# Attention and an MLP on one core: sums of x, stores of weight sums and x's loads are put elsewhere in the queues

## The chip, the cores and the metric

The kernel runs on one core of a Trainium2 chip. The metric is device time in microseconds (us), the median of several runs. A core has five engines that run side by side, each with its own queue of instructions in a fixed order: TensorE (PE; its weight loads are shown apart as PEld), VectorE (DVE), ScalarE (ACT), GpSimd (POOL) and SyncE (SP), which here only issues DMAs. ScalarE and GpSimd issue DMAs too, between their other instructions. An engine waits at the head of its queue until what the next instruction needs is there; everything behind it waits along.

## The reference

What must be computed is an attention whose mask comes from hashes, and an MLP on its output.

```python
# q, k, v: (4, 8, 768, 64); proj: (64, 6); w_in: (512, 2048); w_out: (2048, 512)
q_bits = (np.einsum('bhsd,dk->bhsk', q, proj) > 0)
k_bits = (np.einsum('bhsd,dk->bhsk', k, proj) > 0)
mask = q_bucket[:, :, :, None] == k_bucket[:, :, None, :]      # all six bits equal
scores = np.where(mask, scale * q @ k.T, -1e9)
x = (softmax(scores) @ v)            # to (3072, 512): heads side by side
h = x @ w_in
out = (np.maximum(h, 0) + alpha * np.minimum(h, 0)) @ w_out
```

## The kernel before

**Two parts.** Attention goes over 16 pairs of heads (4 batches of 4 pairs); pair `pi` is one turn of the loop at L1190. It takes the first 320 us or so. Then the MLP runs over 4 batches of x. Its products are cut into blocks of two by two and made with seven products in place of eight, so sums and differences of blocks are needed: of w_in (index `wsi`, kept in the DRAM buffer `w_in_s`), of w_out, of x and of the MLP's inner values g. The sums for the MLP's first batch are made during attention.

**One pair on TensorE.** Twelve cells of scores (L782), each six matmuls: two with the hash bits (`qb`, `kb`), four with q and k. A cell is 128 keys by 384 queries; the cells go key block by key block, and within one over the two halves of the queries, so the first cell needs the bits of k's first half and of q's first half, the second q's second half, and k's second half only from the seventh cell on. Then come the hash products of the next pair (L732), the products with v (L815) and the column sums of the exponentials (L828, tile `sm`). Scores, hash products and column sums share three PSUM buffers (`two_banks`, L691) in turn: a pair's third cell takes the buffer of the last pair's column sums, which VectorE's transpose `st` (L842) must have read; the fourth cell takes the buffer of the first, which ScalarE's exp (L785) must have read.

**Around it.** ScalarE makes the exp of every cell, the signs of the hash products (L736), squares for a check (L719) and parts of the weights' rounding (`weight_abs`, L604 and L608). VectorE adds the exponentials of six key blocks (`add_first`, L793, adds blocks 0 and 1 and so needs four cells' exps; then L801, L797, L798, L804), turns q and k (L712), finishes the last pair's division (`divide`, L832: `st`, reciprocals, `vs`, then the transpose `dn` of `rr`, then x at L860) and rounds the weights (L614, L620, L645, L648). Between the reciprocals and `dn`, GpSimd copies four pieces of `rr` (L851, L852). `divide` of pair `pi - 1` is called behind the scores of pair `pi`; the function `weight_begin` is called inside it, between GpSimd's copies and `dn`, and holds the turn of k, the rounding of a weight piece and `add_first`.

**Sums of w_in.** A group of four rounded pieces gives four sums (`one`, L667, on GpSimd) and four stores (`store`, L672, SyncE). They wait in the list `sums_due`; `weight_sums(1)` takes one sum from it, and is called twice in a pair: within `divide` ahead of the copies of `rr`, and behind the pair's second rounding. A store in the list goes with the next call. There are four such groups.

**DMAs.** The bits of a pair are packed by eight small DMAs from `hr` to `qb` and `kb` (L743): two issued by ScalarE, six by GpSimd. SyncE loads q and k of pair `pi + 3` (L515, four DMAs each), v of pair `pi + 2` (L491), stores x of each pair to DRAM (`x_s`, L861), loads blocks of x (`load_x`, L875) and of w_in's sums (`load_w`, L891) for the MLP.

**Order.** `do(...)` keeps an instruction in program order among those of its engine that are marked so. DMAs without it are placed by the scheduler, as the loads of q, k and v and the stores of w_in's sums here.

Of the kernel before, what the change touches and what calls it, by code (L numbers as in the profile page):

```python
# [407 lines left out]
def fast_path(  # L408
# [12 lines left out]
    nc = tc.nc  # L421
    P = 128
    B, H, S, D = q.shape
    NB = proj.shape[1]
# [4 lines left out]
    NC = S // P  # L429
# [4 lines left out]
    CW = CH * P  # L434
# [8 lines left out]
    do = tc.keep_in_program_order  # L443
    PE, DVE, ACT, POOL = nc.tensor, nc.vector, nc.scalar, nc.gpsimd
# [10 lines left out]
    NPAIR = len(pairs)  # L455
# [18 lines left out]
    w_in_s = dram.tile([NI, P, NM, 2, P], F32, name="w_in_s")  # L474
# [8 lines left out]
    nat, tr, bits = {}, {}, {}  # L483
    accp, accd, av, vsum, sums = {}, {}, {}, {}, {}

    def load(pi, name):
        b, hp = pairs[pi]
        src = {"q": q, "k": k, "v": v}[name]
        if name == "v":
            t = pool.tile([P, 2, NC * D], F32, name=f"vn{pi}", tag="vn")  # L490
            nc.sync.dma_start(t, src[b, 2 * hp : 2 * hp + 2].rearrange("h (p c) d -> p h (c d)", c=NC))  # L491
            nat[name, pi] = t
        elif pi and name in BY_BLOCKS:
            load_blocks(pi, name)
        else:
            load_part(pi, name, slice(0, NC), nc.sync)
# [102 lines left out]
    def weight_abs(i, engine=None):  # L599
        i = order[i]  # L600
        lo, hi = halves(i)
        wx[i] = pool.tile([P, 512], F32, name=f"wx{i}", tag="wx")
        wr[i] = pool.tile([P, 512], I32, name=f"wr{i}", tag="wr")
        do(ACT.activation(wr[i], lo, AF.Copy, scale=2.0 ** -29))  # L604
        if engine is DVE:
            do(DVE.tensor_scalar(wx[i].bitcast(U32), hi, 0x7FFFFFFF, None, op0=ALU.bitwise_and))
            return
        do(ACT.activation(wx[i], hi.bitcast(F32), AF.Abs))  # L608
# [7 lines left out]
    def weight_parts(i):  # L616
        i = order[i]
        x = wx[i].bitcast(U32)
        turned = i < HW and i % 4 == 3
        do(DVE.tensor_scalar(  # L620
            x, x, 3, 0x40000000 if turned else 0xC0000000, op0=ALU.logical_shift_left, op1=ALU.bitwise_xor,
        ))
# [25 lines left out]
        do(DVE.tensor_tensor(dst.bitcast(I32), x, r, op=ALU.add))  # L648
        return (dst if i < HW else dst[:, 0])[:, :1]

    sums_due = []

    def weight_group(i):

        i = order[i]
        if i >= HW:
            n, m = divmod(i - HW, 2)
            if m == 1:
                nc.sync.dma_start(w_out_r[:, :, n].rearrange("m p d -> p m d"), wst[HW + n])
            return  # L660
        n, m = divmod(i, 4)
        if m < 3:
            return
        w = wst[n]

        def one(to, a, op, c):
            do(POOL.tensor_tensor(w[:, to], w[:, a], w[:, c], op=op))  # L667

        def store():
            c, kk = divmod(n, 2)  # L670
            for ii in range(4):
                nc.sync.dma_start(w_in_s[4 * c + ii][:, :, kk], w[:, :, ii])  # L672


        for x in ((3, 5, 2), (5, 0, 5), (4, 3, 0), (6, 1, 4)):
            sums_due.append((one, (x[0], x[1], ALU.subtract, x[2])))
        sums_due.append((store, ()))

    late_sum = const.tile([P, 1], F32, name="late_sum")

    def weight_sums(count, after=None):

        if sums_due and after is not None:
            do(POOL.tensor_copy(late_sum, after))
        while sums_due and count:
            fn, x = sums_due.pop(0)
            count -= fn.__name__ == "one"
            fn(*x)


    def two_banks(name):  # L691
# [34 lines left out]
    def hash_bits(pi):  # L726

        ps = two_banks(f"hs{pi}")[:, 0, :CW]
        for half in range(2):
            for n, name in enumerate("kq"):  # L730
                c = D * n + 32 * half
                do(PE.matmul(  # L732
                    ps[c : c + 32], wh2, tr[name, pi][:, half * CW : (half + 1) * CW], start=True, stop=True,
                ))
        raw = pool.tile([P, CW], BF16, name=f"hr{pi}", tag="hr", bufs=1)
        do(ACT.activation(raw, ps, AF.Sign, bias=hb2))  # L736
        bits["q", pi], bits["k", pi] = qbs[pi % 2], kb
        for half in range(2):
            for n, name in enumerate("kq"):
                for s in range(2):  # L740
                    c = D * n + 32 * half + NB * s
                    queue = nc.gpsimd if half or name == "q" else nc.scalar
                    queue.dma_start(  # L743
                        bits[name, pi][D * s : D * s + 2 * NB, half * CW : (half + 1) * CW], raw[c : c + 2 * NB],
                    )

    def hash_first(half):

# [25 lines left out]
    def scores(pi, cells):  # L774
        for kc, g in cells:
            sc = two_banks(f"sc{pi}_{kc}_{g}")
            ks = slice(kc * P, (kc + 1) * P)
            qs = slice(g * CW, (g + 1) * CW)
            for what, first in ((bits, True), (tr, False)):
                for s in range(2):  # L780
                    r = slice(D * s, D * s + D)
                    do(PE.matmul(  # L782
                        sc[:, s, :CW], what["k", pi][r, ks], what["q", pi][r, qs], start=first, stop=not first,
                    ))
            do(ACT.activation(pts[kc][:, g, :, :CW], sc[:, :, :CW], AF.Exp, scale=SCALE / DOWN))  # L785
# [5 lines left out]
    def add_first(pi):  # L791
        accp[pi] = pool.tile([P, 2 * NCH, CW], F32, name=f"accp{pi}", tag="accp", bufs=1)
        do(DVE.tensor_tensor(accp[pi], p(0), p(1), op=ALU.add))  # L793
# [77 lines left out]
    def load_x(b, *ns):  # L871
        for n in ns or range(4):
            m, kh, ch = ((0, 0, 0), (1, 1, 0), (2, 1, 1), (5, 0, 1))[n]
            t = mid.tile([P, 2, CW], F32, name=f"x{b}_{m}", tag=f"x{m}", bufs=1)
            pinned(b == 0, nc.sync.dma_start(  # L875
                t, x_s[b, 2 * kh : 2 * kh + 2].rearrange("k p s -> p k s")[:, :, ch * CW : (ch + 1) * CW],
            ))
            x_m[b, m] = t

    def sum_x(b, n, engine):  # L880

        to, a, c = ((3, 5, 0), (5, 2, 5), (4, 2, 3), (6, 4, 1))[n]
        if to != 5:
            x_m[b, to] = mid.tile([P, 2, CW], F32, name=f"x{b}_{to}", tag=f"x{to}", bufs=1)
        do(engine.tensor_tensor(x_m[b, to], x_m[b, a], x_m[b, c], op=ALU.subtract))
# [303 lines left out]

    for pi in range(NPAIR):  # L1190
        i = 2 * pi

        def weight_begin():
            if pi == 1:
                turn_blocks(2, "q")
            if pi + 1 < NPAIR:
                turn_blocks(pi + 1, "k")
            weight_clamp(i)
            weight_parts(i)
            add_first(pi)  # L1200

        if pi:
            scores(pi, CELLS)
            divide(pi - 1, weight_begin)
        else:
            rest = [c for c in CELLS if c not in ahead]
            scores(pi, rest[:4])
            weight_abs(0, DVE)
            scores(pi, rest[4:])
            add_first(pi)  # L1210
            weight_clamp(0)
            weight_parts(0)
        if pi in (8, 10, 12, 14):
            sum_x(0, (8, 10, 12, 14).index(pi), DVE)
        weight_sum(i)
        weight_group(i)
        load_weight(i + 3)
        if pi == 0:
            weight_abs(1, DVE)
        weight_clamp(i + 1)  # L1220
        add_third(pi)
        add_last(pi)
        add_total(pi)
        weight_parts(i + 1)
        weight_sums(1, weight_sum(i + 1))
        weight_group(i + 1)
        load_weight(i + 4)
        if pi + 1 < NPAIR:
            hash_bits(pi + 1)
            do(ACT.activation(tr["q", pi + 1], tr["q", pi + 1], AF.Copy, scale=DOWN))  # L1230
        if 0 < pi < NPAIR - 2:
            turn_blocks(pi + 2, "q")
        attend(pi)
        if pi + 1 == NPAIR:
            now = ff1(0, 0)
            now.step(1)
        totals(pi)
        if pi + 1 == NPAIR:
            now.step(5)
            divide(pi)  # L1240
        else:
            weight_abs(i + 2)
        if pi + 2 < NPAIR:
            load(pi + 2, "v")
        if pi in (9, 11, 15):
            load_w((9, 11, 15).index(pi))
        if pi in (5, 6, 8):
            load_x(0, *{5: (0,), 6: (2, 3), 8: (1,)}[pi])
        if pi == 1:
            setup_alpha()  # L1250
        for name in "qk":
            magnitude(pi, name)
            if pi + 3 < NPAIR:
                load(pi + 3, name)
        if pi + 1 < NPAIR:
            weight_abs(i + 3)


# [95 lines left out]
```

## Time and profile before

| | us |
|---|---|
| median of 3 runs | 872.16 (871.22 to 872.3) |
| the profiled execution | 872.62 |
| its span, first to last instruction | 870.8 |
| TensorE busy in the span | 860.5 |
| VectorE busy | 734.2 |
| ScalarE busy | 375.0 |
| GpSimd busy | 119.1 |
| VectorE busy from 200 to 240 | 37.9 of 40 |
| TensorE's clock as granted, mean | 0.998 of full speed |

Span and profiled execution differ by what lies before the first and behind the last instruction. Times in the views of the profile are counted from the span's start. A line of the view in order of time has the start, the duration, the engine, the line of the kernel, the operation, the tiles written and read, the shapes, the number of instructions, and in brackets the idle time ahead of it with what ended it. A line of the view by stretches has the stretch, its length, the busy time and the number of instructions of PE, PEld, DVE, ACT and POOL, the clock, the share of the DMA engines' time that packets took, and GB/s.

### The profile page before, as it was taken

The numbers are of one execution on the slowest core, as the hardware profiler recorded it, in microseconds if no ns is written. First come the engines' busy times: TensorE is split into PE (matmuls) and PEld (weight loads), VectorE is DVE, ScalarE is ACT, GpSimd is POOL, SyncE is SP. The second block draws the span as 40 slices with busy tenths as digits, with TensorE's granted clock in tenths as the row PEclk, the third lists the DMA queues.
The fourth block names the chain that finished last, engine by engine and source line by source line (L and its number), as shares of the span: only waits on it lengthen the run. The fifth ranks groups of instructions, "written<-read, shape, count | busy, mean of one in ns | idle before, by whom it ended". The sixth has DMA issues, their size and how long they took to land.

```text
span 870.8 us, 14641 instructions
## 1 busy us (share of the span) xinstructions
PE 860.5 (99%) x5458; PEld 575.5 (66%) x5458; DVE 734.2 (84%) x1188; ACT 375.0 (43%) x682; POOL 119.1 (14%) x253
## 2 busy tenths in 40 slices
PE   9999999999999999999999999999999999999996
PEld 4444444444445445569985559996558997557996
DVE  6999989999999987899887669897659898568886
ACT  6787878868778733331113331112332112332111
POOL 1322423333435310210000000000000000000001
PEclk9999999999999999999999999999999999999999
DMA  8956796998697446785334335333425433420242
GB/s 197 188 135 130 185 248 176 184 228 207 130 259 177 144 132 236 257 285 222 115 115 121 133 126 165 121 145 92 166 95 163 145 109 115 164 84 1 97 151 72
DMA packets 171104, 135.35 MB, mean 155 GB/s; under 512 B 126240, under 2 KB 155088, under 8 KB 167440
## 3 DMA queue, kind: packets, MB, share of 16 engines
q1 hardware_dynamic: 158528, 108.44, 44.2%
q0 software_dynamic: 9488, 24.56, 9.3%
q10 hardware_dynamic: 3008, 1.33, 0.6%
q8 instruction: 45, 0.74, 0.3%
q14 instruction: 35, 0.29, 0.1%
HBM read 104.87 MB, written 28.31 MB: 153 GB/s over the span
## 4 chain that ended last, share of the span: by engine, by line


## 5 line engine op out<-in xcount | busy, mean ns | idle before, releaser
L782 PE MATMUL sc<-qT,kT 64*128 64x384 f32 x768 | 155.7, 483 | 0.0
L785 ACT ACTIVATE pt<-sc 128x768 f32<-128x768 f32 x192 | 151.5, 811 | 1.2 <-PE sc L782 1.2
L815 PE MATMUL av<-pt,vn 128*32 128x385 f32 (+1 forms) x1536 | 127.0, 485 | 0.0
L815 PEld LDWEIGHTS av<-pt,vn 128*32 128x32 f32 x1536 | 50.3, 109 | 73.8 <-issue 69.8
L782 PEld LDWEIGHTS sc<-qT,kT 64*128 64x128 f32 x768 | 69.2, 187 | 35.0 <-issue 34.0
L975 DVE TENSOR_TENSOR g<-g,g 128x384 f32<-128x384 f32 x128 | 68.3, 554 | 2.2
L1094 POOL DMA_DIRECT2D out_dram<-o x4 | 2.2, 555 | 474.3 <-DVE o L1087 474.3
L782 PE MATMUL sc<-qb,kb 64*128 64x384 bf16 x384 | 65.3, 323 | 1.4 <-ACT pt L785 0.7
L971 DVE SCALAR_TENSOR_TENSOR g<-h,alpha 128x384 f32<-128x384 f32 x60 | 36.8, 614 | 25.2 <-ACT h L964 25.1
L1032 DVE TENSOR_TENSOR ws<-wl 128x512 f32<-128x512 f32 x56 | 38.4, 686 | 21.9 <-DMA wl<-w_out_s 18.0
L1040 DVE TENSOR_TENSOR gs<-g,gs 128x768 f32<-128x768 f32 x56 | 53.3, 952 | 1.0
L1040 DVE TENSOR_TENSOR gs<-g 128x768 f32<-128x768 f32 x56 | 53.2, 950 | 0.0
L782 PEld LDWEIGHTS <-kb 64*128 64x128 bf16 x384 | 21.8, 94 | 36.9 <-issue 13.2
L604 ACT ACTIVATE wr<-raw 128x512 int32<-128x512 uint32 x32 | 22.1, 691 | 35.9 <-DVE wsi L648 18.4
L793 DVE TENSOR_TENSOR accp<-pt,pt 128x1536 f32<-128x1536 f32 x16 | 28.1, 1759 | 8.4 <-ACT pt L785 8.4
L743 POOL DMA_DIRECT2D qb<-hr x60 | 30.1, 507 | 22.8 <-ACT hr L736 22.8
L798 DVE TENSOR_TENSOR accd<-accd,pt 128x1536 f32<-128x1536 f32 x16 | 28.1, 1759 | 1.7
L804 DVE TENSOR_TENSOR accd<-accd,accp 128x1536 f32<-128x1536 f32 x16 | 28.1, 1758 | 0.6
L801 DVE TENSOR_TENSOR accp<-accp,pt 128x1536 f32<-128x1536 f32 x16 | 28.0, 1753 | 0.0
L797 DVE TENSOR_TENSOR accd<-pt,pt 128x1536 f32<-128x1536 f32 x16 | 28.0, 1750 | 0.0
L1230 ACT ACTIVATE qT<-qT 128x768 f32<-128x768 f32 x15 | 12.7, 844 | 26.5 <-DMA kb<-hr 16.4
L915 PE MATMUL f_0a<-x,wi 128*128 128x384 f32 x64 | 23.5, 490 | 0.0
(366 smaller groups left out, 1767.7 us busy)
## 6 DMA issues: line engine op xcount, KB each, us to landing
wi<-w_in_s SPq DMA_DIRECT2D x32, 896.0 KB
wl<-w_out_s SPq DMA_DIRECT2D x16, 1024.0 KB
wl<-w_out_r SPq DMA_DIRECT2D x12, 1024.0 KB
raw<-in_moe_w_in_dram POOLq DMA_DIRECT2D x15, 512.0 KB, 5.2
raw<-in_moe_w_out_dram POOLq DMA_DIRECT2D x14, 512.0 KB, 4.9
w_in_s<-wsi SPq DMA_DIRECT2D x16, 448.0 KB
qn<-in_q_dram SPq DMA_DIRECT2D x64, 96.0 KB
vn<-in_v_dram SPq DMA_DIRECT2D x16, 384.0 KB
```

The lines of the kernel that those rows point to most:

```text
L743: queue.dma_start(bits[name, pi][D * s : D * s + 2 * NB, half * CW : (half + 1) * CW], raw[c : c + 2 * NB],)
L782: do(PE.matmul(sc[:, s, :CW], what["k", pi][r, ks], what["q", pi][r, qs], start=first, stop=not first,))
L785: do(ACT.activation(pts[kc][:, g, :, :CW], sc[:, :, :CW], AF.Exp, scale=SCALE / DOWN))
L793: do(DVE.tensor_tensor(accp[pi], p(0), p(1), op=ALU.add))
L797: do(DVE.tensor_tensor(accd[pi], p(3), p(4), op=ALU.add))
L798: do(DVE.tensor_tensor(accd[pi], accd[pi], p(5), op=ALU.add))
L804: do(DVE.tensor_tensor(accd[pi], accd[pi], accp[pi], op=ALU.add))
L815: do(PE.matmul(av[pi][D * s + t : D * s + t + 32, g, :w], nat["v", pi][:, s, kc * D + t : kc * D + t + 32], pts[kc][:, g, s, :w], start=(k ...
L971: do(DVE.scalar_tensor_tensor(new_g(b, m)[:, i], h, al, h, op0=ALU.mult, op1=ALU.max))
L975: do(DVE.tensor_tensor(new_g(b, to)[:, i], g_m[b, x][:, i], g_m[b, y][:, i], op=ALU.subtract))
L1032: do(DVE.tensor_tensor(t, w2[b, n, x], w2[b, n, y], op=op))
L1040: do(DVE.tensor_tensor(t, g2[b, n, x], g2[b, n, y], op=ALU.subtract))
```

## The change

- The sum of x in pairs 8, 10, 12 and 14 (`sum_x`, L885) moves from behind `divide` into `weight_begin`, ahead of `add_first`.
- A group's stores are no longer entries that wait for the next call of `weight_sums`: behind the fourth sum they go to the list `stores_due`, which is emptied behind the load of v at the end of the pair; from pair 14 on they are issued at once. The stores and the loads of v (from pair 2 on) are marked with `do`.
- The blocks of x are loaded in pairs 4, 5, 7 and 8, one in each, instead of in pairs 5, 6 (two) and 8.
- The DMAs of the hash bits: q's second half is issued ahead of k's second half.
- `weight_abs(3)` moves from the end of pair 0 to behind the first three cells of pair 1.

```diff
@@ load @@
-            nc.sync.dma_start(t, src[b, 2 * hp : 2 * hp + 2].rearrange("h (p c) d -> p h (c d)", c=NC))
+            ins = nc.sync.dma_start(t, src[b, 2 * hp : 2 * hp + 2].rearrange("h (p c) d -> p h (c d)", c=NC))
+            if pi > 1:
+                do(ins)
@@ weight_group, weight_sums @@
-    sums_due = []
+    sums_due, stores_due = [], []
...
-                nc.sync.dma_start(w_in_s[4 * c + ii][:, :, kk], w[:, :, ii])
+                do(nc.sync.dma_start(w_in_s[4 * c + ii][:, :, kk], w[:, :, ii]))
...
-        sums_due.append((store, ()))
+        sums_due.append((stores_due.append, (store,)))
...
+    now_stored = []
...
-        while sums_due and count:
+        while sums_due and (count or sums_due[0][0].__name__ != "one"):
             fn, x = sums_due.pop(0)
             count -= fn.__name__ == "one"
             fn(*x)
+            if now_stored and stores_due:
+                stores_due.pop()()
@@ hash_bits @@
-        for half in range(2):
-            for n, name in enumerate("kq"):
-                for s in range(2):
-                    c = D * n + 32 * half + NB * s
-                    queue = nc.gpsimd if half or name == "q" else nc.scalar
-                    queue.dma_start(
-                        bits[name, pi][D * s : D * s + 2 * NB, half * CW : (half + 1) * CW], raw[c : c + 2 * NB],
-                    )
+        for name, half, queue in (("k", 0, nc.scalar), ("q", 0, nc.gpsimd), ("q", 1, nc.gpsimd), ("k", 1, nc.gpsimd)):
+            for s in range(2):
+                c = D * "kq".index(name) + 32 * half + NB * s
+                queue.dma_start(
+                    bits[name, pi][D * s : D * s + 2 * NB, half * CW : (half + 1) * CW], raw[c : c + 2 * NB],
+                )
@@ the loop over pairs @@
+        if pi == 14:
+            now_stored.append(pi)
...
             weight_parts(i)
+            if pi in (8, 10, 12, 14):
+                sum_x(0, (8, 10, 12, 14).index(pi), DVE)
             add_first(pi)
...
-        if pi:
+        if pi == 1:
+            scores(1, CELLS[:3])
+            weight_abs(3)
+            scores(1, CELLS[3:])
+            divide(0, weight_begin)
+        elif pi:
             scores(pi, CELLS)
             divide(pi - 1, weight_begin)
...
-        if pi in (8, 10, 12, 14):
-            sum_x(0, (8, 10, 12, 14).index(pi), DVE)
...
             load(pi + 2, "v")
+        while stores_due and pi < 14:
+            stores_due.pop(0)()
...
-        if pi in (5, 6, 8):
-            load_x(0, *{5: (0,), 6: (2, 3), 8: (1,)}[pi])
+        if pi in (4, 5, 7, 8):
+            load_x(0, {4: 0, 5: 3, 7: 2, 8: 1}[pi])
...
-        if pi + 1 < NPAIR:
+        if 0 < pi < NPAIR - 1:
             weight_abs(i + 3)
```

## The prediction

> **What bounds the kernel.** I read the page first.
>
> ```profile
> PE 860.5 (99%) x5458; PEld 575.5 (66%) x5458; DVE 734.2 (84%) x1188; ACT 375.0 (43%) x682; POOL 119.1 (14%) x253
> ```
>
> TensorE is busy in 860.5 of 870.8 us, and the change removes no matmul. All that it can win are stretches in which TensorE stands, and these must be looked for one by one, because a matmul's modelled end covers much of a stall. So the next view is TensorE's instructions in order of time. An undisturbed cell of scores (six matmuls, L782) starts 0.81 us after the one before, an undisturbed pair's twelve cells take 9.79. I compared all sixteen pairs with that.
>
> ```profile
> 220.74 0.34 PE L782 MATMUL sc<-qb,kb 64*128 64x384 bf16 x2
> 221.56 0.33 PE L782 MATMUL sc<-qb,kb 64*128 64x384 bf16 x2
> 222.74 0.34 PE L782 MATMUL sc<-qb,kb 64*128 64x384 bf16 x2 [0.21 <-DVE st L842]
> ...
> 124.71 0.64 PE L782 MATMUL sc<-qb,kb 64*128 64x384 bf16 x2
> 125.79 0.58 PE L782 MATMUL sc<-qb,kb 64*128 64x384 bf16 x2
> 126.81 0.38 PE L782 MATMUL sc<-qb,kb 64*128 64x384 bf16 x2
> ```
>
> In pair 11 the third cell starts 1.18 after the second: 0.37 lost. In pair 6 the steps are 1.08 and 1.02: 0.48 lost, and 0.10 more ahead of the first cell. Read so, these pairs lose: pair 1 0.54 (fourth cell; waits for ScalarE's exp), pair 6 0.6 (hash bits), pair 9 0.61 (bits at its second cell, st at its third), pair 11 0.37 and pair 13 0.37 (st, third cell), pair 15 0.45 (exp, fourth cell) and 0.13 ahead of its column sums at 296.80. The sum, 3.1 us, is the ceiling of this change; all other pairs run at 9.79. Behind attention one wait is left (1.1 us at 443.77, a load of w_out's blocks), which the change doesn't touch.
>
> **Sums of x (L885).** In pairs 8, 10, 12, 14 such a sum stands behind the store of x; VectorE's order then runs without a gap to the next pair's st (L842), which frees the score bank that the third cell needs.
>
> ```profile
> 204.92 0.43 DVE L620 TENSOR_SCALAR wx<-wx 128x512 uint32<-128x512 uint32 x1
> 206.06 1.76 DVE L793 TENSOR_TENSOR accp<-pt,pt 128x1536 f32<-128x1536 f32 x1 [0.71 <-ACT pt L785]
> 209.67 0.95 DVE L885 TENSOR_TENSOR x<-x,x 128x768 f32<-128x768 f32 x1
> ```
>
> A sum holds the next instruction up by 0.87 (209.67 to 210.54). In pairs 7 and 9, without a sum, st comes 1.0 earlier against the column sums than in pair 8. Moved in front of L793, the sum falls into VectorE's wait for exp: 0.58, 0.71, 0.25 and 0.23 us in pairs 8, 10, 12, 14. That much would be saved, if nothing else were late. But GpSimd copies rr four times (L851, L852) just there, and the transpose dn waits for the last. Pair 11 shows what two-input additions do to these copies:
>
> ```profile
> 225.31 0.19 POOL L852 COPY rr<-rr 32x12 f32<-32x12 f32 x1
> 225.54 1.72 POOL L851 COPY rr<-rr 32x12 f32<-32x12 f32 x1
> 227.30 0.19 POOL L852 COPY rr<-rr 32x12 f32<-32x12 f32 x1
> ...
> 225.44 1.76 DVE L793 TENSOR_TENSOR accp<-pt,pt 128x1536 f32<-128x1536 f32 x1 [0.22 <-ACT pt L785]
> 227.52 0.98 DVE L854 STREAM_TRANSPOSE dn<-rr 128x768 f32<-128x768 f32 x1 [0.32 <-POOL rr L852]
> ```
>
> A copy of 0.19 us takes 1.72 when L793 starts before it, and ends with it; dn starts 0.40 after it could (225.44 + 1.68 = 227.12). In pairs 8, 10 and 14 GpSimd first does a sum of w_in (1.28 us, L667) and comes to the copies at 166.59, 205.10, 282.21, just when x's sum will now start. The sum and L793 follow without a gap, so copies are locked out twice. Pair 8: sum 166.93, L793 167.80, its end for dn 169.48. With two copies left behind L793 dn starts 0.40 later, 169.88; with all four (0.23 apart) and none let in between, 0.86 + 0.2 = 1.1 later, 170.3. L645 came 2.80 after dn and comes 1.93 after it now: 171.8 to 172.25, against 171.98 before. So pair 8 saves between 0.18 and -0.25; the same sum gives 0.30 to -0.16 for pair 10 and 0.23 to -0.23 for pair 14. In pair 12 there is no L667 ahead of the copies and they end at 243.5, before the sum: 0.25 is saved. I take one copy let in at each boundary, since nothing shows who goes first there: 0.0, 0.12, 0.25, 0.05. **Sum 0.42**, bounds -0.4 and 0.96.
>
> The Trainium skill (SBUF — State Buffer, Who interferes with whom) says that an addition with two SBUF inputs shuts out GpSimd reads for the whole instruction, and that whoever issues first holds the port. By issue order a waiting copy would go ahead of the next addition, which gives 0.42; no run yet shows that boundary.
>
> **Stores of w_in's sums (L672).** Four DMAs, some 4.3 us of SyncE's issue, 1.8 MB. They leave now at 114.1, 171.7, 251.9 and 300.0. The fourth sum is done at 108.9, 166.5, 241.8 and 300.0, so behind v's load they leave at 124.5, 182.0, 242 and, in pair 14 at once, 300.0. The first two then no longer stand in front of the bits that hash_bits sends at 116.96 and 174.51. In the trace's packets those bits first move at 122.1 and 179.6, 5.1 us after the issue, and land 0.3 and 0.2 us before their cells; in pairs 2 to 4 and 6, without stores, they first move after 1.4. So pair 6's 0.6 us go: **0.6 saved**, between 0 and 0.63. Pair 9's bits wait goes too, but its third cell is set by st (184.39), so nothing is counted there twice. Sending q's second half ahead of k's helps the same cells, brings it 1 us forward, and hides in the same way.
>
> The Trainium skill (DMA: Bandwidth & Descriptors, Queues, rings and completion order) says that each DMA engine takes turns between queues packet by packet. By it bits in another queue would not wait for stores, and this part would save nothing (total 0.4); the 5.1 us speak against it.
>
> What is late next: the moved stores take 6.5 us of the 16 engines (3584 packets of 29 ns on average), now ahead of q's and k's loads on SyncE.
>
> ```profile
> 124.60:144.20 19.60, 19.57 (x188) 10.03 (x184) 17.90 (x25) 15.14 (x23) 4.92 (x14) 1.00 0.67 163
> 182.20:201.80 19.60, 19.48 (x190) 9.26 (x188) 18.93 (x27) 15.02 (x23) 5.55 (x14) 1.00 0.82 189
> 240.10:259.10 19.00, 19.00 (x190) 9.04 (x188) 18.37 (x26) 14.80 (x22) 6.20 (x15) 1.00 1.04 256
> ```
>
> The DMA share (last but one) is 0.67 and 0.82 in the pairs that get them, plus 0.34. The bits of pairs 6, 9 and 12 moved at 137.95, 197.52 and 254.1; their cells start at 144.21, 201.76, 259.09 and need some 1.6 us from first packet to semaphore. If the bits slip by about half of 6.5, because k's loads are issued after them, the spare is 3.0, -0.7 and 1.7. Pair 10 may lose some tenths; q's half going earlier gives 0.5 to 1 of it back. Taken as 0, bounds 0 and 6.3 (rival B).
>
> **x's loads** (384 KB) become one per pair, in pairs 4, 5, 7, 8. Each is needed two pairs on at the earliest (8). Cover: pair 4's DMA is idle at 100 to 103. 0. v's pinning: it already stands there, 0.
>
> **weight_abs(3).** Two activations, 30.00 to 31.14, stand ahead of pair 1's first exp and make it 1.1 late. Behind three cells they start at 32.42 (the exp of the third cell starts 1.03 after it, at 31.66, and takes 0.76), so the fourth exp ends at 34.37 instead of 33.25, and the seventh cell, due at 33.87, needs its bank: 0.53 late instead of 0.54. **0.02 saved**, bounds 0 and 0.1. The wait moves.
>
> **Sum.** 0.42 + 0.6 + 0.02 = 1.05. From the profiled execution's 872.62: 871.6; that run lies 0.46 above the median of the three shown (872.16), so **871.1**. This case's own range: 870.4 (0.96 + 0.63 + 0.1) to 872.2.
>
> **Rivals.** A: GpSimd's copies don't hold VectorE up, or are through before. Then the waits absorb the sums in full: 0.58, 0.37, 0.25, 0.55, with pair 6 and pair 1 2.4 in all: 869.8. For it: the copies need only 0.9 us. Against: three locked copies of 1.7 us in pairs 11, 13, 14.
> B, slower: bits and k late behind the moved stores. A slip of the full 6.5 makes pair 7 lose 1.8, pair 10 1.3 (its q half landing last) and pair 13 3.1: +6.2 - 1.05, 877.3; a slip of 5 makes about half of that, 874. It decides from a slip of some 4 us, where 1.05 is eaten. For it: DMA share above 1 in pairs 9 and 12. Against: SyncE issues k's loads behind the stores, hence behind the bits.
> C: the stores moved, but pair 6's wait stays (another cause): 871.7.
>
> **Chances.** Forecast 0.42, A 0.27, B 0.21, C 0.10. A measurement of this kernel tells about 0.2% (1.7 us, 870.4) from no change. Faster by more: A and a third of the forecast, 0.40; slower by more: most of B, 0.21; within 0.39. Range 869.4 to 874.2: A's time less 0.4 for the wait in the late part, and B at a slip of 5.
>
> **What would show it.** Right: pair 6 at 9.79; st of pairs 9 and 11 within 0.2 of before; copies L851 of 1 to 2 us in pairs 8, 10, 14; pair 1's seventh cell 0.5 late. Wrong: any of pairs 7, 10, 13 waiting for qb or kb, or k's turn (L712) waiting near 261.5.

## The result and the profile after

The kernel after the change takes 873.2 us (median, 871.7 to 875.75), the kernel before 871.76 in the runs beside it (870.75 to 873.2). The ratio is 1.002, with an interval of 1.0011 to 1.0029: the change makes the kernel 0.2% slower, where 871.1 was forecast, about 1 us faster. The profiled execution took 872.97, and the page's first part reads:

```profile
span 871.2 us, 14629 instructions
PE 859.3 (99%) x5458; PEld 574.3 (66%) x5458; DVE 733.7 (84%) x1188; ACT 375.2 (43%) x682; POOL 121.5 (14%) x249
```

Nothing is to be seen there: busy times differ from before by little over 1 us on TensorE and by 2.4 on GpSimd, whose copies now wait. So I compare again pair by pair on TensorE, from a pair's first matmul of scores to the next pair's. A pair without a wait takes 18.98 us; pair 15 has nothing to prepare for the next and would take about 17.7. The table adds what goes beyond that, one profiled execution each.

| excess, us | pairs 1, 2 | pairs 3 to 12 | pairs 13 to 15 | first cell of pair 1 to the MLP's first product |
|---|---|---|---|---|
| before | 0.72 | 1.61 | 1.00 | 286.75 |
| after | 0.96 | 0.05 | 2.68 | 287.11 |

Pairs 3 to 12 lost 1.61 and now lose nothing, more than I forecast. Pairs 13 to 15 lose 2.68 in place of 1.00, and that eats it. Between these two executions the stretch from pair 1 to the MLP differs by 0.36 only, the medians by 1.44. Before was profiled once, in an execution of 872.62, which lies 0.86 above its median and holds a wait in the MLP that the profile of after doesn't have (last section); what else makes up the 1.44 isn't shown. TensorE's instructions of these pairs in order of time show where, after the change:

```profile
258.21 0.74 PE L786 MATMUL sc<-qb,kb 64*128 64x384 bf16 x2
259.36 0.39 PE L786 MATMUL sc<-qb,kb 64*128 64x384 bf16 x2
260.81 0.34 PE L786 MATMUL sc<-qb,kb 64*128 64x384 bf16 x2 [0.41 <-DVE st L846]
...
278.13 0.85 PE L832 MATMUL sm<-accd,ones 128*32 128x384 f32 x8 [0.54 <-DVE accd L808]
...
281.18 0.34 PE L786 MATMUL sc<-qb,kb 64*128 64x384 bf16 x2 [0.47 <-DVE st L846]
```

Cells that follow each other without a wait start 0.81 apart. In pair 13 the second starts 1.15 after the first (by k's bits: the first cell's second hash product waits for `kb` until 258.61) and the third 1.45 after the second, waiting for `st`; at the pair's end the column sums wait for VectorE's last addition, and pair 14's third cell for `st` again. One delay on VectorE shows up three times. VectorE's own order has its origin:

```profile
257.80 0.69 DVE L650 CUSTOM_DVE_ANT_0 wsi<-wx,wr 128x1024 uint16<-128x1024 uint16 x1
259.31 0.98 DVE L718 STREAM_TRANSPOSE qT<-qn 128x768 f32<-128x768 f32 x1 [0.82 <-DMA qn<-in_q_dram]
260.21 0.54 DVE L846 STREAM_TRANSPOSE st<-sm 128x384 f32<-128x384 f32 x1
...
263.44 0.98 DVE L718 STREAM_TRANSPOSE kT<-kn 128x768 f32<-128x768 f32 x1 [2.11 <-DMA kn<-in_k_dram]
```

The turns of q and k of pair 14 wait 0.82 and 2.11 us for their loads. `st` stands behind the first, everything else of the pair behind the second. Before, the same two turns start without a wait:

```profile
259.61 0.97 DVE L712 STREAM_TRANSPOSE qT<-qn 128x768 f32<-128x768 f32 x1
...
261.52 0.97 DVE L712 STREAM_TRANSPOSE kT<-kn 128x768 f32<-128x768 f32 x1
```

And SyncE's queue (start and duration of the issue) shows why these loads are late, first after, then before:

```profile
240.54 1.65 SPq L491 DMA_DIRECT2D vn<-in_v_dram  x1
242.29 5.81 SPq L674 DMA_DIRECT2D w_in_s<-wsi  x4
248.15 0.70 SPq L895 DMA_DIRECT2D wi<-w_in_s  x1
248.89 1.86 SPq L517 DMA_DIRECT2D qn<-in_q_dram  x2
250.85 8.29 SPq L517 DMA_DIRECT2D kn<-in_k_dram  x4
```

```profile
243.15 0.66 SPq L891 DMA_DIRECT2D wi<-w_in_s  x1
243.85 1.72 SPq L515 DMA_DIRECT2D qn<-in_q_dram  x2
245.66 6.12 SPq L515 DMA_DIRECT2D kn<-in_k_dram  x4
251.88 6.14 SPq L672 DMA_DIRECT2D w_in_s<-wsi  x4
```

Before, the third group's stores followed the loads of q and k. After, these four DMAs (1.8 MB) stand ahead of them, together with the block of w_in's sums (0.9 MB), which stood there before as well. k's issue begins 5.2 us later and ends 7.4 later (251.78 against 259.14). Without a wait the turn that needs k would start at about 260 (259.96 in held3 below).

### The profile page after: what moved, and what is told of

Its sections match the earlier page's. It is cut to its first block, busy times and chain, and to the rows that moved or that the text cites. A ratio compares the mean times of both kernels' runs of the same rounds, so it can differ in the third digit from the quotient of the medians.

```text
span 871.2 us, 14629 instructions
## 1 busy us (share of the span) xinstructions
PE 859.3 (99%) x5458; PEld 574.3 (66%) x5458; DVE 733.7 (84%) x1188; ACT 375.2 (43%) x682; POOL 121.5 (14%) x249
## 4 chain that ended last, share of the span: by engine, by line
## 5 line engine op out<-in xcount | busy, mean ns | idle before, releaser
L797 DVE TENSOR_TENSOR accp<-pt,pt 128x1536 f32<-128x1536 f32 x16 | 28.1, 1756 | 6.1 <-ACT pt L789 6.1
```

## The experiments

First the question was whether the third group's stores, ahead of q and k of pair 14, cost what the rest gains, or whether another part makes the loss. So parts were tried alone, and the third group apart.

### The third group's stores one pair later (held3)

```diff
+            while stores_due and pi == 12:
+                stores_due.pop(0)()
...
-        while stores_due and pi < 14:
+        while stores_due and pi < 14 and pi != 11:
```

> The changed kernel, but the third group's four stores wait for the middle of pair 12, about where the kernel before has them; nothing else differs. Theory Q (these stores, ahead of w_in's block and of q and k on SyncE at 242, make q and k of pair 14 late, VectorE's turns wait 0.8 and 2.1 us, and pairs 13 to 15 lose what the rest wins): pairs 13, 14 and 15 give back about 2.4 us of the changed kernel's 3.0 (13: 20.71 to about 19.1, 14: 19.63 to 19.0, 15 unchanged or shorter), no wait of the turn of k near 261; time 2 to 2.5 below the changed kernel, some 870.5 to 871. Theory D (VectorE's new order in pairs 12 and 14 is what makes them long): lengths of pairs 13 and 14 stay within 0.3 and the time stays near 873.

Measured: 870.95 us, ratio to before 0.9986 (0.9976 to 0.9997), 2.3 below after. Pairs 13 to 15 lose 0.31 in place of 2.68. SyncE's queue and the two turns:

```profile
242.43 1.91 SPq L517 DMA_DIRECT2D qn<-in_q_dram  x2
244.44 5.77 SPq L517 DMA_DIRECT2D kn<-in_k_dram  x4
...
251.00 6.79 SPq L674 DMA_DIRECT2D w_in_s<-wsi  x4
```

```profile
258.04 0.97 DVE L718 STREAM_TRANSPOSE qT<-qn 128x768 f32<-128x768 f32 x1
...
259.96 0.97 DVE L718 STREAM_TRANSPOSE kT<-kn 128x768 f32<-128x768 f32 x1
```

No bracket stands behind the turns: nothing is waited for. So the slowdown is this one group's place, and without it the change is a gain.

### The moved stores alone (stores)

The kernel before, with the new place of the stores and the pinned load of v, and nothing else.

```diff
-        sums_due.append((store, ()))
+        sums_due.append((stores_due.append, (store,)))
...
+        while stores_due and pi < 14:
+            stores_due.pop(0)()
```

> The kernel before, with the moved stores and the pinned loads of v alone. Theory Q: pair 6 loses its 0.5 us wait for bits, pairs 9 and 11 keep their wait for st (0.4 to 0.6), and pairs 13 to 15 become at least as long as in the changed kernel (13 near 20.7 or more, since the sums of x still stand late): some 1.5 to 3 us slower than before, 873.5 to 875. Theory D: pairs 13 and 14 as before (19.4, 19.1), time 0.5 below before.

Measured: 873.86, ratio 1.0021 (1.0012 to 1.0031). The whole loss is in this part: pairs 13 to 15 lose 3.58, and k's turn waits longest of all.

```profile
264.15 0.98 DVE L717 STREAM_TRANSPOSE kT<-kn 128x768 f32<-128x768 f32 x1 [2.69 <-DMA kn<-in_k_dram]
```

Pairs 3 to 12 lose 0.78 against 1.61: the first two groups, moved in the same way, take pair 6's wait away and put none in its place.

### The sums of x alone (sums)

```diff
             weight_parts(i)
+            if pi in (8, 10, 12, 14):
+                sum_x(0, (8, 10, 12, 14).index(pi), DVE)
             add_first(pi)
...
-        if pi in (8, 10, 12, 14):
-            sum_x(0, (8, 10, 12, 14).index(pi), DVE)
```

> The kernel before, with the sums of x ahead of the first addition alone. If the sums win what the changed kernel's trace shows: pairs 11, 13 and 15 lose their waits of 0.38, 0.38 and 0.46, pair 9 keeps only its wait for bits (0.25 to 0.4), pair 6 stays at 19.5; 1.3 to 1.7 us faster than before, near 870.3. By the prediction's term: 0.4 faster, pairs 9 and 11 keep 0.3 or more each.

Measured: 871.46, ratio 0.9988 (0.9978 to 0.9998). From pair 1's first cell to the MLP 285.37 us, 1.38 less than before. Pairs 9, 11, 13 run within 0.06 of 18.98, and pair 15 loses 0.25 in place of 0.46. Pair 6's wait (0.6) stays, as it must. Pair 9's bits, expected 0.25 to 0.4 late, are in time here, though the stores still stand ahead of them. The times can't tell 0.4 from 1.4 saved (the ratio's interval is 0.2 to 1.9 us, and the median is above the 870.3 expected); the lengths of the pairs do.

### weight_abs(3) at its old place (abs_back)

```diff
-        if pi == 1:
-            scores(1, CELLS[:3])
-            weight_abs(3)
-            scores(1, CELLS[3:])
-            divide(0, weight_begin)
-        elif pi:
+        if pi:
...
-        if 0 < pi < NPAIR - 1:
+        if pi + 1 < NPAIR:
             weight_abs(i + 3)
```

> The changed kernel with weight_abs(3) at its old place, ahead of pair 1's first exp. The wait goes back from pair 1's seventh cell to its fourth (0.49 to 0.54) and pair 2 loses the 0.3 that it has in the changed kernel: together 0.1 to 0.3 faster than the changed kernel. If the part were what makes the changed kernel slower, the time would fall by 1 us or more.

Measured: 873.8, ratio 1.0018 (1.0009 to 1.0028), against 1.002 for after: this part doesn't make the loss, and in the time it can't be told from nothing. The pairs tell more: pairs 1 and 2 lose 0.72 as before, 0.96 with the move, since pair 2's second cell then starts 0.29 late. This kernel's profiled execution took 875.31, and three things add up in it: pairs 3 to 12 lost 1.02 (0.3 in pair 9; 0.7 at the end of pair 12, where the next pair's bits come late), pairs 13 to 15 2.94, and the MLP ran 1.56 us longer than in after.

### The same stores in the same pair, behind q and k (qk_first)

Held back by a whole pair, the stores also meet other traffic. Is it the queue's order or the amount of traffic? Here they leave in pair 11 still, at its end.

```diff
-        while stores_due and pi < 14:
+        while stores_due and pi < 14 and pi != 11:
             stores_due.pop(0)()
...
                 load(pi + 3, name)
+        while stores_due and pi == 11:
+            stores_due.pop(0)()
```

> The kernel after, with the third group's four stores issued in the same pair (11), but behind the loads of q and k of pair 14 on SyncE. Same bytes in the same pair; only the order on SyncE differs. Theory Q (the order in SyncE's queue decides: q and k for the next turn land late because the stores stand ahead of them): k's turn (L718) at about 260 without a wait, as in held3, pairs 13 and 14 at 19.04 and 18.98, pair 15 at 18.0, median 870.9 (870.3 to 871.4), 2.3 below after. Rival T (the amount of traffic in that stretch decides, wherever it stands in the queue): k's packets and the bits of pair 13 share the 16 engines with the 1.8 MB as before, k's turn waits for 1 us or more, pair 13 at 20.0 or more, median 872.3 to 873.3. If T holds in part: the bits of pair 13 (sent at about 252) are late in its first cells by up to 0.6, since the stores are now issued at about 251 to 257, just in front of them.

Measured: 871.13, ratio 0.9991 (0.9983 to 1.0), 2 us below after. Both turns start without a wait (258.2 and 260.1), pairs 13 and 14 take 18.98, pair 15 loses 0.11. The order decides; rival T falls, and the bits of pair 13, sent beside the stores, have all moved by 257.9, and pair 13's first cell starts undisturbed at 258.43. Pair 11 lost 0.57 in this execution, ahead of the place where the kernels differ: its first cell waits for k's bits, which ScalarE issued 1.5 us later than in held3 (213.70 against 212.24).

### The block of w_in one pair later, the stores where after has them (wi_late)

```diff
-        if pi in (9, 11, 15):
-            load_w((9, 11, 15).index(pi))
+        if pi in (9, 12, 15):
+            load_w((9, 12, 15).index(pi))
```

> The kernel after, with the load of w_in's second block (load_w(1), 896 KB) moved from pair 11 to pair 12; the third group's stores stay behind v in pair 11, ahead of the loads of q and k. Theory Q says that the third group alone is late because 1.8 MB of stores and 0.9 MB of this load stand together ahead of q and k: without the load q and k are issued 0.75 earlier and wait for one third less. k's turn waited 2.11 and q's 0.82 in after; 0.9 MB is some 3.3 us of 16 engines by the stores' rate (1.8 MB in 6.5), so k's wait goes to 0 and so do pair 13's and 14's losses: median 871.0 (870.4 to 871.6). Rival S (the stores alone are enough to make k late, the block's load adds nothing): k's turn waits for 1.4 or more, median 872.6 to 873.4. In between (k's turn waiting 0.2 to 1): 871.6 to 872.4.

Measured: 869.87, 1.1 below what was expected, but the ratio, 0.9986 (0.9975 to 0.9996), is that of held3; pair 13 loses 0.08, pair 14 nothing. The stores stand ahead of q and k as in after, and neither turn waits:

```profile
241.76 6.24 SPq L674 DMA_DIRECT2D w_in_s<-wsi  x4
248.05 2.17 SPq L517 DMA_DIRECT2D qn<-in_q_dram  x2
250.33 5.53 SPq L517 DMA_DIRECT2D kn<-in_k_dram  x4
```

So rival S falls too: the stores alone don't make k late, the stores and the block together do. Against pair 13's first cell (257.50 here, 258.21 in after) k's issue even starts 0.2 later, but it takes 5.53 instead of 8.29. Three of the twelve times lie at 872.2 to 873.0, and no profile has caught such a one.

### The order of the bits and the loads of x undone (bits_x_back)

held3 with the hash DMAs in their old order and x loaded in pairs 5, 6 (two) and 8.

```diff
-        for name, half, queue in (("k", 0, nc.scalar), ("q", 0, nc.gpsimd), ("q", 1, nc.gpsimd), ("k", 1, nc.gpsimd)):
+        for half in range(2):
+            for n, name in enumerate("kq"):
...
-        if pi in (4, 5, 7, 8):
-            load_x(0, {4: 0, 5: 3, 7: 2, 8: 1}[pi])
+        if pi in (5, 6, 8):
+            load_x(0, *{5: (0,), 6: (2, 3), 8: (1,)}[pi])
```

> held3 with two parts of the change undone: the DMAs that send the hash bits in their old order (q's second half last), and x loaded as before in pairs 5, 6 (two) and 8. If these parts are worth nothing, as predicted: 870.95 as held3 (870.3 to 871.6), pairs 3 to 12 within 0.1 of 18.98 each. If the order of the bits matters: pairs 6, 9 or 12 show a bits wait of 0.2 to 0.6 at their first or second cell, 871.3 to 872.2. If the loads of x matter: pair 6 or 7's bits 0.1 to 0.5 late behind the two loads in pair 6.

Measured: 870.75, ratio 0.9989 (0.998 to 0.9998) against held3's 0.9986: no difference. No cell waits for bits from pair 3 on. Pair 11's third cell is 0.24 late, by `st`: a step of the rounding ahead of it (L647) took 0.87 us where held3 has 0.69. These two parts are worth nothing that could be measured.

### held3 with weight_abs(3) at its old place (held3_abs)

Both edits above, held3's and abs_back's, together.

> held3 with weight_abs(3) back where it stood before the change. Expected as the best version here: pair 1's wait stays 0.54 (fourth cell in place of the seventh, 0.49), pair 2's 0.29 goes, so 0.25 less than held3: 870.7 (870.0 to 871.4), 1.1 below before, 2.5 below after. If the move of weight_abs is worth what the prediction said (0.02 gained), it is 870.97, the same as held3; a difference of 0.25 is near what the comparison can tell, so the pair lengths decide: pair 2 at 18.98 (theory) or 19.28 (not).

Measured: 870.2, ratio 0.9983 (0.9975 to 0.9992), and pair 2 takes 18.98. Its ratio is the lowest that was measured, 0.17% below before, and its median 3 us below after; from held3 and wi_late (0.9986 both) it can't be told apart. From pair 1's first cell to the MLP it takes 284.54; without any wait it would be 283.4 (14 times 18.98, and 17.7).

### The kernel after, three times more (after_2, after_3, after_4)

Five of the 17 times of after lie at 874.8 to 875.8. The kernel was profiled again as it is, to see what such an execution holds.

> The kernel after, unchanged, to see another execution: five of its 17 times lie at 874.8 to 875.8, the others at 871.7 to 874. Expected if this one falls in the higher group: the 2.5 us more stand in pairs 12 to 15 (k's turn waiting 4 us or more in place of 2.11, pair 13 at 22 or more), since that is where the loads run late; rival: in the late part, where one wait of about 1 us came and went between executions of other kernels (late part 548 or more in place of 546.9). If it falls in the lower group: pair 13 between 20 and 21.5 and k's turn waiting 1 to 3.

> As after_2: the same kernel again. k's turn waits in pair 13 in every execution (1 us or more), pair 13 is 20 or longer; a time above 874.5 comes with pair 13 at 22 or more (or, by the rival, with a late part of 548 or more).

> As after_2 and after_3: the same kernel again; the time of each execution less 872.97 should be the sum of what pairs 12 to 15, the first pair and the late part differ by from the first profile.

Measured: 872.99, 872.59 and 873.64; none was of the higher ones. The wait is there each time:

| | q's turn waits | k's turn waits | pairs 13 to 15 lose | pairs 3 to 12 lose | MLP, first to last product |
|---|---|---|---|---|---|
| after | 0.82 | 2.11 | 2.68 | 0.05 | 546.87 |
| after_2 | 1.79 | 1.44 | 2.35 | 0.69 | 547.04 |
| after_3 | 1.04 | 2.49 | 3.27 | 0.04 | 546.75 |
| after_4 | 1.39 | 1.46 | 2.45 | 0.14 | 548.20 |

Here after_2 loses 0.6 at the end of pair 12 to late bits, and after_4 1.4 in the MLP. What makes up an execution of 875 was seen only in abs_back, a sum of such waits; for after itself it stays open.

## Why the prediction was wrong

**What bounds the kernel** was read rightly: the waits of TensorE, pair by pair, with a ceiling of 3.1 us (3.3 by the lengths of the pairs: 0.72, 1.61 and 1.00). held3_abs comes to 2.2 of them (286.75 less 284.54).

**Sums of x**: right in sign, sized too small, 0.42 against 1.38. GpSimd's copies did just what I assumed, one let in at each boundary of two additions. GpSimd and VectorE in pair 8 of after:

```profile
166.57 0.36 POOL L855 COPY rr<-rr 32x12 f32<-32x12 f32 x1
166.98 0.83 POOL L856 COPY rr<-rr 32x12 f32<-32x12 f32 x1
167.85 1.63 POOL L855 COPY rr<-rr 32x12 f32<-32x12 f32 x1
169.52 0.19 POOL L856 COPY rr<-rr 32x12 f32<-32x12 f32 x1
```

```profile
166.80 0.95 DVE L889 TENSOR_TENSOR x<-x,x 128x768 f32<-128x768 f32 x1
167.68 1.75 DVE L797 TENSOR_TENSOR accp<-pt,pt 128x1536 f32<-128x1536 f32 x1
169.74 0.98 DVE L858 STREAM_TRANSPOSE dn<-rr 128x768 f32<-128x768 f32 x1 [0.32 <-POOL rr L856]
170.76 1.02 DVE L864 SCALAR_TENSOR_TENSOR x<-av,vs,dn 128x768 f32<-128x768 f32 x1
171.69 0.68 DVE L647 SCALAR_TENSOR_TENSOR wx<-raw,wx 128x512 uint32<-128x512 uint32 x1
```

A copy of 0.19 us takes 0.83 and 1.63, each until the addition beside it ends, and the last comes behind both. The lock-out was right; my price for it was too high. The sum starts at 166.80, not 166.93, and `dn` at 169.74, not 169.88. L647 follows at 171.69, where its like stood at 171.98 before: 0.29 earlier on the clock, and 0.35 against pair 9's first cell, which starts 0.06 later than before. I had 0.18 at best and took 0.0. Behind it, the next rounding step took 0.69 us instead of 0.90, so `st` of pair 9 came 0.56 earlier against that cell (183.30 and 182.23 after, 183.80 and 182.17 before), and its third cell no longer waits. Why that step was shorter isn't shown, but moving the sums isn't the reason: in stores, where the sums of x stand as before, it takes 0.69 too. So 0.21 of the 1.38 isn't this part's. In sums the waits of pairs 9, 11, 13 shrink by 0.57, 0.39 and 0.34 and those of pairs 14 and 15 by 0.36 (pairs 5 and 6 lose 0.26 more in that execution), which is near rival A's amounts, though not by rival A's reason, since the copies do hold `dn` up. The Trainium skill (SBUF — State Buffer, Who interferes with whom) says that issue order decides which engine holds the shared port. The trace agrees: the copy of 166.98, which comes behind the sum of 166.80, is through at 167.81, just past the sum's end, and the copy of 167.85, behind L797, at 169.48, just past that one's.

**Stores, first two groups**: right. I said 0.6; the runs with the stores moved lose 0.8 to 0.9 less in pairs 3 to 12 (0.78 against 1.61 in stores, 0.03 in held3 against 0.92 in sums). Rival C, that pair 6's wait stays, is refuted. What recurs is the first group's: pairs 5 and 6 together lose 0.62 in before and 0.88 in sums, and nothing in any of the eleven profiles with the stores moved. The rest of stores' gain is pair 9 (0.39 for 0.61), where the shorter rounding step of above stands. Its bits are late in before but not in sums, so what the second group's move is worth isn't shown.

**What is late next**: here it failed. I took the slip as 0 and argued against rival B that SyncE issues k's loads behind the stores, hence behind the bits, as a relief for the bits. That k's own load has a due time two pairs on, I named only as a sign (the turn near 261.5) and gave no price. The spare of that load is what a moved DMA uses up. I also took the stores' issue as some 4.3 us, which the second group's was; the third's took 6.14 before and 5.81 after, and k's issue was put off by 5.2. For the bits, the spares that I gave at half the slip (3.0, -0.7, 1.7) don't come out of the numbers beside them, which give 1.4, -0.6 and 0.1, and the full slip gives 3.9 for pair 10 by the same working, where I put 1.3. Pair 13 had next to nothing to spare. The bits of pairs 7, 10 and 13 first moved 2.3, 2.2 and 4.0 after their issue in after (1.4, 3.4 and 2.7 before), so only pairs 7's and 13's slipped, by 0.9 and 1.4. SyncE's queue of after at the first two groups, and VectorE's turns of the same k:

```profile
125.24 6.24 SPq L674 DMA_DIRECT2D w_in_s<-wsi  x4
...
134.71 6.50 SPq L517 DMA_DIRECT2D kn<-in_k_dram  x4
...
182.18 6.23 SPq L674 DMA_DIRECT2D w_in_s<-wsi  x4
...
191.84 6.03 SPq L517 DMA_DIRECT2D kn<-in_k_dram  x4
```

```profile
145.91 0.97 DVE L718 STREAM_TRANSPOSE kT<-kn 128x768 f32<-128x768 f32 x1
...
202.85 0.97 DVE L718 STREAM_TRANSPOSE kT<-kn 128x768 f32<-128x768 f32 x1
```

k's issue ends at 141.21 and 197.87, the turns stand 4.7 and 5.0 us later, and nothing waits. With the third group the issue ends at 259.14, and the turn, 1.9 behind q's, would start at about 260. The trace of before had these due times and showed that, of the three, only the third group has a block's load between it and q and k. Its price is 2.37 in the profiled executions (2.68 less held3's 0.31).

**Rival B**'s mechanism came true in part: at pair 13, not at 7 and 10, and by k more than by the bits. Its price for pair 13 was 3.1; 2.4 was measured over pairs 13 to 15. That the time still lies in my range (869.4 to 874.2) is due to this rival, not to the forecast, which had the sign wrong.

**weight_abs(3)**: the wait moved from the fourth cell to the seventh as I said (0.54 to 0.49). But pair 2's second cell is 0.29 late too, so the 0.02 gained is 0.2 lost.

**x's loads, the order of the bits**: nothing, as said. v's pinning wasn't tried by itself.

**The sum by parts**, from pair 1's first cell to the MLP: 1.38 (sums of x) + 0.89 (0.92 less 0.03, first two groups) - 2.37 (third group) - 0.24 (0.96 less 0.72, weight_abs) = -0.34. Measured was 286.75 less 287.11, which is -0.36. This holds for the profiled executions, not for the medians. My own sum had slips too: its terms add to 1.04, and by their bounds this case's range ends at 872.6, not at 872.2.

**The named signs**: pair 6 at its undisturbed length, pair 1's seventh cell 0.5 late and copies of 1 to 2 us in pairs 8, 10, 14 came as said. `st` of pairs 9 and 11 came earlier by more than 0.2. And two signs for wrong, a wait at k's turn and pair 13 waiting for `kb`, are what the trace shows.

## What to carry to other kernels

A DMA that is moved forward in a queue moves everything behind it back, so for each of those, look up who waits for it, when it is issued, and when it is needed; the least spare decides, not the first consumer that comes to mind. Do it for each place where the moved work occurs: three groups went the same way, the first for a gain, the second without a loss, and the third, with another large load behind it, cost more than all else gained. When a change of several parts ends near zero, try the parts alone: here two were worth 0.9 and up to 1.4 us by the profiles, and one cost 2.4.

## What was unexpected on the chip

An issue can take long on SyncE, and the engines may be empty by the time it ends. In after, the four loads of k were issued one by one at 250.85, 254.60, 257.47 and 258.17: the first two issues held SyncE for 3.70 and 2.83 us, the others for 0.66 and 0.97. In held3 and wi_late only one of the four is so long (3.32 and 3.16). The view of DMA activity of after, from 238 to 264, in 40 slices of 0.65 us:

```profile
DMA  2109747999999999999999989999941974699999
GB/s 33 25 0 126 82 120 296 359 383 322 339 359 342 347 347 347 347 347 347 371 378 397 353 290 385 373 234 204 113 61 24 137 118 85 235 315 312 353 346 230
```

The stores move at 347 GB/s (about 246 to 250), the block's load behind them. At 113 GB/s (256.2 to 256.85) they are still at least 90% busy, with small packets; but from 256.85 to 258.15 they are busy for 0.4 and 0.1 of the time, at 61 and 24 GB/s: the engines ran nearly dry while the third of k's loads was being issued and the fourth was still to come. So k was late by the time that its issue was held up as well as by the bytes ahead of it. What holds an issue up, no run here shows. Counted by size, the packets on SyncE's queue moved in the order of issue: stores (512 bytes) from 245 to 251, the block (7168) from 250 to 255, q's and k's (128) from 253 to 262.7. The Trainium skill (DMA: Bandwidth & Descriptors, Queues, rings and completion order) says that a ring's descriptors are consumed in order, which agrees.

A load on another queue stands in k's way too. GpSimd issues the load of a piece of w_out (512 KB, packets of 4096 bytes) just ahead of the last of k's loads:

```profile
258.06 0.54 POOL L592 DMA_DIRECT2D raw<-in_moe_w_out_dram  x1 [4.26 <-DVE wx L647]
```

Its packets move from 260.03 to 262.08, and between 260.17 and 261.49 no packet of k's moves at all; those of k's last load, issued at 258.17, come from 261.49 to 262.70, and the turn starts at 263.44. In wi_late the last of k's loads is issued at 255.11, ahead of this load (257.35), and nothing waits. It looks as if the late issue cost more than its own delay, because this load went first. How much of the 2.4 us is due to that isn't shown, since no run moved this load.

A second thing is the spread. The MLP, with the same instructions, took 546.75 us in nine of thirteen profiled executions to within 0.3 and 547.8 to 548.4 in the four others (before, held3, abs_back, after_4). In before it is one wait for a load of w_out's blocks. Such a wait comes and goes between executions of one kernel, so a difference of 1 us between two of them says nothing; the lengths of the pairs do.
